# Folding the last two token blocks into a pair of seven half products

## The chip, the cores and the metric

The kernel runs on one core of a Trainium2 chip. The metric is the device time of one execution in microseconds (us). "Span" is the time from the first to the last instruction in a profile; the times of whole runs lie about 1.7 us above it. A store is "issued" when an engine's instruction starts it and "landed" when the profile shows that its data have arrived. An "eviction" is the instruction that reads a finished product out of its accumulator ("bank") so that it can be stored.

## The reference, cut to what matters

Eight batches of a linear attention of eight heads give 4608 tokens of 512 features; a bilinear layer follows.

```python
def _moe_ref(x, w_a, w_b, w_out):
    a = x @ w_a
    b = x @ w_b
    return (a * b @ w_out).astype(np.float32)   # 4608 x 1536  by  1536 x 512
```

The change concerns only the last product. Its left side, `a * b`, is kept transposed in fp16 as `ht`, and it is worked off in 36 blocks of 128 tokens.

## The kernel before

Blocks 0 to 3 are multiplied plainly, early. Then two blocks at a time are multiplied with seven groups of half products in place of eight (a Strassen-like scheme). A half product is one matmul of 256 columns, and each of the seven groups is six of them. The scheme needs four sums of weights, made once, and four sums of tokens per pair (`h_sums`), made on GpSimd, for the last pair on VectorE. Only blocks 4 to 33 are paired. At the end stand block 34 plainly, the last pair (32, 33), and block 35 in two column halves. The code is shortened.

```python
def last_down(cidx):
    for x in range(2):
        cs = slice(w * x, w * (x + 1))
        ...  # 12 matmuls of 256 columns into one bank
        nc.scalar.mul(out=o_sb[:, :w // 2], in_=po[:, :w // 2], mul=1.0 / (CS * CS))
        nc.vector.tensor_scalar(out=o_sb[:, w // 2:], in0=po[:, w // 2:], ...)
        for z, engine in enumerate((nc.sync, nc.scalar)):
            engine.dma_start(out=out_rows[..., cs], in_=o_sb[64 * z:64 * z + 64, :])

def two_downs(self, cidx):              # one pair; self is the work list
    ...
    yield from products(y, a11, quarter(0, 0), True);  u1 = part(y, "u1")     # group 1
    yield from products(v, S1, T1, True);              u5 = part(v, "u5")     # group 2
    yield from products(y, S2, T2);                    u2 = part(y, "u2")     # group 3
    yield from products(v, S4, quarter(1, 1));         plus(o1[:, NH:], v, u2)
    yield from products(y, S3, T3);                    plus(o2[:, NH:], y, u5)
    yield from products(x, a12, quarter(1, 0), True);  plus(o1[:, :NH], x, u1)
    store(o1, cidx)
    yield from products(y, a22, T4)                                           # group 7
    nc.scalar.mul(out=o2[:, :NH], in_=y, mul=scale)
    store(o2, cidx + 1)

def products(self):                     # of class Work: the order of the work
    for cidx in PAIRED[:-1]:
        yield from two_downs(self, cidx)
    yield from down(BLOCKS - 2)
    yield from two_downs(self, PAIRED[-1])
```

`part` is an eviction on ScalarE, `plus` one on VectorE. Note that group 7 adds to the bank `y` that `plus(o2[:, NH:], y, u5)` has to have read. The token sums are put into an engine's order 24 half products ahead of their use (`LEAD`).

The softmax here doesn't subtract the row's maximum and nothing guards it: scores larger than these inputs give would overflow.

Of the kernel before, what the change touches and what calls it, by code (L numbers as in the profile page):

```python
# [8 lines left out]
F32 = mybir.dt.float32  # L9
F16 = mybir.dt.float16  # L10
AF = mybir.ActivationFunctionType
ALU = mybir.AluOpType

P = 128
CS = 16.0
# [3 lines left out]
def kernel(  # L19
# [11 lines left out]
    nc = tc.nc  # L31

    B, H, S, D = q.shape
    M = phi.shape[3]
    d_model, d_ff = moe_w_a.shape
    NHP = H // 2
    NI = S // 64
    NFF = d_ff // P
# [12 lines left out]
    opool = ctx.enter_context(tc.tile_pool(name="opool", bufs=4))  # L51
# [15 lines left out]
    wo_sb = wpool.tile([P, NFF, d_model], F16, name="wo_sb")  # L67
# [72 lines left out]
    banks = Banks()  # L140
# [238 lines left out]
    ht = consts.tile([P, NFF, 2 * S], F16, name="ht")  # L379
    out_rows = out.rearrange("(b p i) f -> b i p f", b=B, i=NI)  # L380

    def down_part(po, bank, cidx, lo, hi):
        pair, c = divmod(cidx, NI)
        for i in range(lo, hi):
            nc.tensor.matmul(po, ht[:, i, P * c:P * (c + 1)], wo_sb[:, i, :],  # L385
                             start=(i == 0), stop=(i == NFF - 1))
            if i == NFF - 1:
                banks.free(bank)
                o_sb = opool.tile([P, d_model], F32, name="o_sb")
                nc.scalar.mul(out=o_sb, in_=po, mul=1.0 / (CS * CS))  # L390
                for z in range(2):
                    slot = 2 * c + z
                    nc.sync.dma_start(out=out_rows[2 * pair + slot // NI, slot % NI],
                                      in_=o_sb[64 * z:64 * z + 64, :])
            yield

    def down(cidx):

        po, bank = banks.take([P, d_model], F32, "po", hold=True)
        yield from down_part(po, bank, cidx, 0, NFF)  # L400

    def last_down(cidx):

        pair, c = divmod(cidx, NI)
        w = d_model // 2
        for x in range(2):
            cs = slice(w * x, w * (x + 1))
            po = banks.tile([P, w], F32, name="pl")
            o_sb = opool.tile([P, w], F32, name="o_sb")
            for i in range(NFF):  # L410
                nc.tensor.matmul(po, ht[:, i, P * c:P * (c + 1)], wo_sb[:, i, cs],
                                 start=(i == 0), stop=(i == NFF - 1))
            nc.scalar.mul(out=o_sb[:, :w // 2], in_=po[:, :w // 2], mul=1.0 / (CS * CS))
            nc.vector.tensor_scalar(out=o_sb[:, w // 2:], in0=po[:, w // 2:], scalar1=1.0 / (CS * CS), scalar2=None,
                                    op0=ALU.mult)
            for z, engine in enumerate((nc.sync, nc.scalar)):
                slot = 2 * c + z
                engine.dma_start(out=out_rows[2 * pair + slot // NI, slot % NI, :, cs],
                                 in_=o_sb[64 * z:64 * z + 64, :])

    EARLY = 4

    def early_downs():
# [9 lines left out]
    KH = NFF // 2  # L433
    NH = d_model // 2
    w_sums = wpool.tile([P, 4, KH, NH], F16, name="w_sums")

    def quarter(x, y):
        return wo_sb[:, KH * x:KH * (x + 1), NH * y:NH * (y + 1)]
# [13 lines left out]
    def sum_tokens(cidx, engine):  # L452

        h_sums[cidx] = spool.tile([P, 4, KH, P], F16, name="h_sums")
        t = [h_sums[cidx][:, x] for x in range(4)]
        (a11, a12), (a21, a22) = ([tokens_of(cidx + y, x) for x in range(2)] for y in range(2))
        for out, in0, in1, op in ((t[0], a21, a22, ALU.add), (t[1], t[0], a11, ALU.subtract),
                                  (t[2], a12, t[1], ALU.subtract), (t[3], a11, a21, ALU.subtract)):
            engine.tensor_tensor(out=out, in0=in0, in1=in1, op=op)  # L459
            yield  # L460

    def store(o_sb, cidx):
        pair, c = divmod(cidx, NI)
        for z in range(2):
            slot = 2 * c + z
            nc.sync.dma_start(out=out_rows[2 * pair + slot // NI, slot % NI], in_=o_sb[64 * z:64 * z + 64, :])

    def two_downs(self, cidx):
        S1, S2, S4, S3 = (h_sums[cidx][:, x] for x in range(4))
        T1, T2, T3, T4 = (w_sums[:, x] for x in range(4))  # L470
        (a11, a12), (a21, a22) = ([tokens_of(cidx + y, x) for x in range(2)] for y in range(2))
        scale = 1.0 / (CS * CS)

        def products(po, lhs, rhs, first=False):
            for i in range(KH):
                nc.tensor.matmul(po, lhs[:, i], rhs[:, i], start=first and i == 0,  # L476
                                 stop=i == KH - 1, skip_group_check=not first)
                if i < KH - 1:
                    yield

        def part(po, name):
            x = ppool.tile([P, NH], F32, name=name)
            nc.scalar.mul(out=x, in_=po, mul=scale)
            return x

        def plus(o, po, x):
            nc.vector.scalar_tensor_tensor(out=o, in0=po, scalar=scale, in1=x, op0=ALU.mult, op1=ALU.add)

        o1, o2 = (opool.tile([P, d_model], F32, name="o_sb") for _ in range(2))
        y, ybank = banks.take([P, NH], F32, "py", hold=True)  # L490
        yield from products(y, a11, quarter(0, 0), True)
        u1 = part(y, "u1")
        yield
        v, vbank = banks.take([P, NH], F32, "pv", hold=True)
        self.brim = True
        yield from products(v, S1, T1, True)
        u5 = part(v, "u5")
        yield
        yield from products(y, S2, T2)
        u2 = part(y, "u2")  # L500
        yield
        yield from products(v, S4, quarter(1, 1))
        banks.free(vbank)
        plus(o1[:, NH:], v, u2)
        self.brim = False
        yield
        yield from products(y, S3, T3)
        plus(o2[:, NH:], y, u5)
        yield
        x, xbank = banks.take([P, NH], F32, "px", hold=True)  # L510
        self.brim = True
        yield from products(x, a12, quarter(1, 0), True)
        banks.free(xbank)
        plus(o1[:, :NH], x, u1)
        store(o1, cidx)
        self.brim = False
        yield
        yield from products(y, a22, T4)
        banks.free(ybank)
        nc.scalar.mul(out=o2[:, :NH], in_=y, mul=scale)  # L520
        store(o2, cidx + 1)
        yield

    BLOCKS = B // 2 * NI
    LEAD = 24
    PLAIN = 0
    PAIRED = range(EARLY + PLAIN, BLOCKS - 2, 2)

    class Work:

# [7 lines left out]
            self.next_sum = next(self.sums)  # L538

        def products(self):  # L540
            for cidx in range(EARLY, EARLY + PLAIN):
                yield from down(cidx)
            for cidx in PAIRED[:-1]:
                yield from two_downs(self, cidx)
            yield from down(BLOCKS - 2)
            yield from two_downs(self, PAIRED[-1])

        def add_up(self):
            for n, cidx in enumerate(PAIRED):
                for x in range(4):  # L550
                    yield n, NFF * PLAIN + 7 * KH * n + KH * (x + 1)
                    if x == 0:
                        sums = sum_tokens(cidx, nc.gpsimd if n < len(PAIRED) - 1 else nc.vector)
                    next(sums)
            while True:
                yield len(PAIRED), 0

# [21 lines left out]
        def plan(self, tokens, slots, keep=24):  # L579

            n = min(max(0, tokens // P - PAIRED[0]) // 2, len(PAIRED))
            self.summed = n
            self.ready = NFF * min(PLAIN, tokens // P - EARLY) + 7 * KH * n + NFF * (tokens // P >= BLOCKS - 1)
            self.rate = max(0, self.ready - self.done - keep) / slots
            self.owed = 0.0
            self.sum_ahead()
# [78 lines left out]
    def chain(b, plan):  # L665


        for x in plan.split():
            if x[0] == "f":
                fill(int(x[1:]), 256)  # L670
            elif x[0] == "y":
                some(int(x[1:]))
            else:
                us[b][x]()
# [4 lines left out]
    ups(steps(0, 0, 4), slots(0, "- hv1a+hx1a - hv1b+hx1b - v1a+x1a - v1b+x1b"))  # L679
    load(2)  # L680
    ups(steps(0, 4, 12), slots(0, "- - - - v2a+x2a - v2b+x2b"))
    chain(1, "exp0 exp1 y9 ks0 y3 kt0 qt0 qt1 y1 ks1 y3 kt1 s0 e0 qt2 qt3 y6 den0 y2 s1 e1 nr0 y4 den1 y2 vs0 vs1 y1 vt0 vt1 nr1 y1 "
             "hv0a hx0a y2 hv0b hx0b y2")
    load(3)
    sum_weights()
    ups(steps(1, 0, 4), slots(1, "y1 hv1a+hx1a hv1b+hx1b y1 v1a+x1a v1b+x1b y3 y3"))
# [13 lines left out]
            ups(half_steps(b, hf), side[NFF * hf:NFF * (hf + 1)] if hf == 0 else side[NFF:])  # L700
    work.plan(S * B, 1, 0)
    work.pull(work.ready - work.done)
    last_down(B // 2 * NI - 1)
# [1 line left out]
_INS = ['q', 'k', 'v', 'phi', 'moe_w_a', 'moe_w_b', 'moe_w_out']  # L705
_OUTS = [((4608, 512), 'float32')]
# [25 lines left out]
```

## Time and profile before

| | before |
|---|---|
| time, median of 3 | 248.29 us (247.92 to 248.95) |
| span of the profiled run | 246.7 us |
| TensorE busy | 95% |
| TensorE's last product ends | 242.23 us |
| last store issued, landed | 243.51, 245.52 us |

The prediction below shows the lines. From 231.5 us on TensorE works without a gap up to its last product, but 4.5 us pass between that product (242.23) and the end (246.74), and in them a queue of stores decides: its last store had its data at 242.93 and was issued at 243.51.

### The profile page before, as it was taken

To read this page: it belongs to the slowest core of one execution; us is meant where nothing else is said; L and a number is where in the kernel's file an instruction comes from. 1 tells how busy PE (TensorE), PEld (TensorE's weight loads), DVE (VectorE), ACT (ScalarE), POOL (GpSimd) and SP (SyncE) were. 2 spreads that over 40 slices of the span, in tenths; PEclk is the share of its full clock that TensorE was granted. 3 is DMA by queue.
4 is the path that set the end of the run, shared out by engine and by line. 5 is a ranking of instruction groups with operands and counts; after the bars stand their busy time and mean duration, and the time that the engine had idled before them with its cause. 6 is when DMAs were issued, how large, how long until landed. Compare 5 with 4: busy or idle time off the path is not lost.

```text
span 246.7 us, 7678 instructions
## 1 busy us (share of the span) xinstructions
PE 235.3 (95%) x3049; PEld 167.3 (68%) x3049; DVE 166.1 (67%) x400; ACT 158.1 (64%) x409; POOL 151.6 (61%) x124
## 2 busy tenths in 40 slices
PE   7989899999998999999999999999999999999992
PEld 2555464456655857777788777877787787888782
DVE  7247773477959967876994649865985676756620
ACT  4147761578697489578856768588855877465230
POOL 8834233499799029892889759892839186946000
PEclk9999999999999999999999999999999999999999
DMA  7999999999979804973159732695120303033145
GB/s 150 196 198 206 207 256 207 255 222 269 235 195 208 159 4 109 234 129 85 34 150 207 173 85 45 168 206 144 36 51 4 86 12 76 15 74 77 43 99 126
DMA packets 26036, 33.53 MB, mean 136 GB/s; under 512 B 1936, under 2 KB 20624, under 8 KB 26000
## 3 DMA queue, kind: packets, MB, share of 16 engines
q0 software_dynamic: 19552, 23.01, 51.2%
q1 hardware_dynamic: 6288, 9.90, 16.3%
q8 instruction: 24, 0.39, 0.6%
q10 hardware_dynamic: 160, 0.13, 0.2%
q14 instruction: 12, 0.10, 0.1%
HBM read 42.47 MB, written 9.44 MB: 210 GB/s over the span
## 4 chain that ended last, share of the span: by engine, by line
PE 74%; DMA 17%; DVE 3%; POOL 2%; issue 1%; ACT 1%; ACTq 0%; DVEq 0%; POOLq 0%
PE pa L598 18%; PE pb L608 16%; PE py L476 15%; PE pv L476 8%; DMA phi_sb<-in_phi_dram 6%; DMA wo_sb<-in_moe_w_out_dram 6%; PE pva L331 5%; DMA wb_sb<-in_moe_w_b_dram 5%; PE px L476 4%; PE po L385 3%; PE pkv L207 2%; PE pD L308 1%; PE pscore L286 1%; PE pT L236 1%; DVE A L319 1%
## 5 line engine op out<-in xcount | busy, mean ns | idle before, releaser
L611 DVE TENSOR_TENSOR ht<-a_sb,pb 128x288 f16<-128x288 f16 x192 | 82.9, 448 | 40.4 <-ACT a_sb L601 29.5
L601 ACT CAST a_sb<-pa 128x288 f16<-128x288 f32 x192 | 74.8, 405 | 31.3 <-PE pa L598 30.7
L598 PE MATMUL pa<-A,vab 128*128 128x288 f16 x384 | 76.6, 287 | 1.4 <-DVE A L319 1.4
L608 PE MATMUL pb<-A,vab 128*128 128x288 f16 x384 | 76.3, 286 | 0.2
L459 POOL TENSOR_TENSOR h_sums<-ht 128x768 f16<-128x768 f16 x28 | 45.8, 1638 | 34.0 <-DVE ht L611 34.0
L608 PEld LDWEIGHTS <-vab 128*128 128x128 f16 x384 | 37.0, 98 | 13.0 <-issue 1.9
L598 PEld LDWEIGHTS <-vab 128*128 128x128 f16 x384 | 34.5, 98 | 15.8 <-issue 9.1
L476 PEld LDWEIGHTS <-h_sums 128*128 128x128 f16 x360 | 35.1, 98 | 6.5 <-issue 0.4
L343 ACT CAST vab<-pva 128x512 f16<-128x512 f32 (+1 forms) x52 | 28.1, 558 | 11.8 <-PE pva L331 11.8
L343 DVE CAST vab<-pva 128x512 f16<-128x512 f32 (+1 forms) x52 | 32.8, 644 | 4.0 <-PE pva L331 3.6
L476 PEld LDWEIGHTS <-ht 128*128 128x128 f16 x270 | 26.4, 98 | 5.4 <-issue 0.2
L476 PE MATMUL py<-w_sums,h_sums 128*128 128x256 f16 x180 | 28.5, 272 | 0.0
L459 POOL TENSOR_TENSOR h_sums<-h_sums,ht 128x768 f16<-128x768 f16 x14 | 23.1, 1647 | 1.0
L459 POOL TENSOR_TENSOR h_sums<-ht,h_sums 128x768 f16<-128x768 f16 x14 | 23.0, 1640 | 1.0
L299 ACT ACTIVATE E<-pscore 128x288 f16<-128x288 f32 x32 | 11.4, 417 | 14.5 <-PE pscore L286 14.4
L319 POOL TENSOR_TENSOR A<-E,R 128x576 f16<-128x576 f16 x10 | 12.8, 1276 | 12.0 <-ACT R L317 11.7
L385 PE MATMUL po<-wo_sb,ht 128*128 128x512 f16 x60 | 16.0, 381 | 0.3 <-DMA wo_sb<-in_moe_w_out_dram 0.3
L476 PE MATMUL py<-wo_sb,ht 128*128 128x256 f16 x90 | 15.2, 273 | 0.0
L476 PE MATMUL pv<-w_sums,h_sums 128*128 128x256 f16 x90 | 15.2, 273 | 0.0
L198 DVE STREAM_TRANSPOSE qT<-q_sb 128x288 f32<-128x288 f32 x32 | 14.5, 463 | 1.0 <-DMA q_sb<-in_q_dram 1.0
L476 PE MATMUL py<-w_sums,ht 128*128 128x256 f16 x90 | 14.7, 272 | 0.1
L476 PE MATMUL px<-wo_sb,ht 128*128 128x256 f16 x90 | 14.6, 273 | 0.0
(64 smaller groups left out, 271.2 us busy)
## 6 DMA issues: line engine op xcount, KB each, us to landing
out_dram<-o_sb SPq DMA_DIRECT2D x70, 128.0 KB, 2.4
kv_sb<-in_v_dram POOLq DMA_DIRECT2D x7, 576.0 KB, 10.0
phi_sb<-in_phi_dram POOLq DMA_DIRECT2D x7, 576.0 KB, 4.6
kv_sb<-in_k_dram POOLq DMA_DIRECT2D x7, 576.0 KB, 8.8
q_sb<-in_q_dram POOLq DMA_DIRECT2D x6, 576.0 KB, 12.7
wo_sb<-in_moe_w_out_dram POOLq DMA_DIRECT2D x3, 512.0 KB, 16.6
q_sb<-in_q_dram POOLq DMA_DIRECT2D x4, 288.0 KB, 12.6
wa_sb<-in_moe_w_a_dram POOLq DMA_DIRECT2D x2, 512.0 KB, 14.9
```

What stands on the lines that cost most here:

```text
L198: nc.vector.transpose(out=t["qT"][:, hp, :].bitcast(F32), in_=qs[b][:, hp, :].bitcast(F32))
L299: nc.scalar.activation(out=Ev[:, g, :, z, :], in_=pss, func=AF.Exp, scale=1.0 / (8.0 * CS))
L319: engine.tensor_tensor(out=attn[b][:, g, sl], in0=t["E"][:, g, sl], in1=t["R", g][:, sl], op=ALU.mult)
L331: nc.tensor.matmul(t["pva", lo, z][g][0][32 * j:32 * j + 32, 0:hi - lo], t["kvT"][64 * r:64 * r + 64, 4 + g, M * j:M * j + M], w_sbs[z][64 ...
L343: engine_copy(out=vabs[b][z][:, g, lo:hi], in_=pva[:, 0:hi - lo])
L385: nc.tensor.matmul(po, ht[:, i, P * c:P * (c + 1)], wo_sb[:, i, :], start=(i == 0), stop=(i == NFF - 1))
L459: engine.tensor_tensor(out=out, in0=in0, in1=in1, op=op)
L476: nc.tensor.matmul(po, lhs[:, i], rhs[:, i], start=first and i == 0, stop=i == KH - 1, skip_group_check=not first)
L598: nc.tensor.matmul(pa, vab[0][:, g, fs], A[:, g, HALF * hf:HALF * (hf + 1)], start=(g == 0), stop=(g == 1))
L601: nc.scalar.copy(out=a_sb, in_=pa)
L608: nc.tensor.matmul(pb, vab[1][:, g, fs], A[:, g, HALF * hf:HALF * (hf + 1)], start=(g == 0), stop=(g == 1))
L611: nc.vector.tensor_tensor(out=ht[:, i, t0:t0 + HALF], in0=a_sbs[hf - hfs[0]], in1=pb, op=ALU.mult)
```

## The change

Blocks 34 and 35 become a sixteenth pair. TensorE has 84 half products at the end in place of 12 full ones, 42 half ones and 24 half ones. The sums of both last pairs are on VectorE. The stores of block 35 go by column halves: the right half after group 5, the left half at the end. The diff is shortened.

```diff
-    def last_down(cidx):
-        ... (block 35 in two column halves)
@@ two_downs
+        ends = cidx == PAIRED[-1]
         yield from products(y, S3, T3)
         plus(o2[:, NH:], y, u5)
+        if ends:
+            store(o2, cidx + 1, slice(NH, d_model))
@@
         nc.scalar.mul(out=o2[:, :NH], in_=y, mul=scale)
-        store(o2, cidx + 1)
+        if ends:
+            store(o2, cidx + 1, slice(0, NH), (nc.sync, nc.scalar))
+        else:
+            store(o2, cidx + 1)
@@
-    PAIRED = range(EARLY + PLAIN, BLOCKS - 2, 2)
+    PAIRED = range(EARLY, BLOCKS, 2)
@@ products: pairs only, block 34 is no longer plain
@@ add_up
-                        sums = sum_tokens(cidx, nc.gpsimd if n < len(PAIRED) - 1 else nc.vector)
+                        sums = sum_tokens(cidx, nc.gpsimd if n < len(PAIRED) - 2 else nc.vector)
@@
-    last_down(B // 2 * NI - 1)
```

More of the change, by code (lines that the diff above doesn't have):

```diff
@@ L400, in down @@
         yield from down_part(po, bank, cidx, 0, NFF)
-    def last_down(cidx):
-        pair, c = divmod(cidx, NI)
-        w = d_model // 2
-        for x in range(2):
-            cs = slice(w * x, w * (x + 1))
-            po = banks.tile([P, w], F32, name="pl")
-            o_sb = opool.tile([P, w], F32, name="o_sb")
-            for i in range(NFF):
-                nc.tensor.matmul(po, ht[:, i, P * c:P * (c + 1)], wo_sb[:, i, cs],
-                                 start=(i == 0), stop=(i == NFF - 1))
-            nc.scalar.mul(out=o_sb[:, :w // 2], in_=po[:, :w // 2], mul=1.0 / (CS * CS))
-            nc.vector.tensor_scalar(out=o_sb[:, w // 2:], in0=po[:, w // 2:], scalar1=1.0 / (CS * CS), scalar2=None,
-                                    op0=ALU.mult)
-            for z, engine in enumerate((nc.sync, nc.scalar)):
-                slot = 2 * c + z
-                engine.dma_start(out=out_rows[2 * pair + slot // NI, slot % NI, :, cs],
-                                 in_=o_sb[64 * z:64 * z + 64, :])
     EARLY = 4
@@ L460, in sum_tokens, with store @@
             yield
-    def store(o_sb, cidx):
+    def store(o_sb, cidx, cs=slice(0, d_model), engines=(nc.sync, nc.sync)):
         pair, c = divmod(cidx, NI)
@@ L465, in store @@
             slot = 2 * c + z
-            nc.sync.dma_start(out=out_rows[2 * pair + slot // NI, slot % NI], in_=o_sb[64 * z:64 * z + 64, :])
+            engines[z].dma_start(out=out_rows[2 * pair + slot // NI, slot % NI, :, cs], in_=o_sb[64 * z:64 * z + 64, cs])
     def two_downs(self, cidx):
@@ L525 @@
     LEAD = 24
-    PLAIN = 0
-    PAIRED = range(EARLY + PLAIN, BLOCKS - 2, 2)
+    PAIRED = range(EARLY, BLOCKS, 2)
     class Work:
@@ L540, in products @@
         def products(self):
-            for cidx in range(EARLY, EARLY + PLAIN):
-                yield from down(cidx)
-            for cidx in PAIRED[:-1]:
+            for cidx in PAIRED:
                 yield from two_downs(self, cidx)
-            yield from down(BLOCKS - 2)
-            yield from two_downs(self, PAIRED[-1])
         def add_up(self):
@@ L550, in add_up @@
                 for x in range(4):
-                    yield n, NFF * PLAIN + 7 * KH * n + KH * (x + 1)
+                    yield n, 7 * KH * n + KH * (x + 1)
                     if x == 0:
-                        sums = sum_tokens(cidx, nc.gpsimd if n < len(PAIRED) - 1 else nc.vector)
+                        sums = sum_tokens(cidx, nc.gpsimd if n < len(PAIRED) - 2 else nc.vector)
                     next(sums)
@@ L582, in plan @@
             self.summed = n
-            self.ready = NFF * min(PLAIN, tokens // P - EARLY) + 7 * KH * n + NFF * (tokens // P >= BLOCKS - 1)
+            self.ready = 7 * KH * n
             self.rate = max(0, self.ready - self.done - keep) / slots
@@ L681 @@
     ups(steps(0, 4, 12), slots(0, "- - - - v2a+x2a - v2b+x2b"))
-    chain(1, "exp0 exp1 y9 ks0 y3 kt0 qt0 qt1 y1 ks1 y3 kt1 s0 e0 qt2 qt3 y6 den0 y2 s1 e1 nr0 y4 den1 y2 vs0 vs1 y1 vt0 vt1 nr1 y1 "
-             "hv0a hx0a y2 hv0b hx0b y2")
+    chain(1, "exp0 exp1 y9 ks0 y3 kt0 qt0 qt1 y1 ks1 y3 kt1 s0 e0 qt2 qt3 y6 den0 y2 s1 e1 nr0 y4 den1 y2 vs0 vs1 y1 vt0 vt1 nr1 y1 hv0a hx0a y2 hv0b hx0b y2")
     load(3)
```

## The prediction

"Instruction" is the profile's name for the packets of q8. That these are TensorE's and are placed by its instruction count is an estimate of mine, from 24 packets of 16 KB for 3049 matmuls and 3049 weight loads. Counted, it holds only roughly: neighbouring packets are 136 to 394 apart.

> **What bounds the kernel now.** I read the page first: busy shares, the slices, the chain.
>
> ```profile
> span 246.7 us, 7678 instructions
> PE 235.3 (95%) x3049; PEld 167.3 (68%) x3049; DVE 166.1 (67%) x400; ACT 158.1 (64%) x409; POOL 151.6 (61%) x124
> PEclk9999999999999999999999999999999999999999
> PE 74%; DMA 17%; DVE 3%; POOL 2%; issue 1%; ACT 1%; ACTq 0%; DVEq 0%; POOLq 0%
> ```
>
> TensorE is 95% busy at full clock and carries 74% of the chain. The change acts only after the last token is known, so I compared the two kernels' instruction orders: up to the 24 half products left over from earlier pairs they are the same on every engine. Only the last 15 us matter. Next I read the chain of waits over that stretch (start, duration, what):
>
> ```profile
> 231.54 0.81 PE py L476 x6
> 232.35 2.59 PE po L385 x12
> 234.94 0.66 PE py L476 x6
> ...
> 238.28 0.66 PE px L476 x6
> 238.94 0.68 PE py L476 x6
> 239.61 1.32 PE pl L411 x12
> ...
> 242.33 0.29 ACT o_sb L413
> 242.61 0.02 issue
> 242.64 0.29 DVE o_sb L414
> ```
>
> The reader should see TensorE without a gap: block 34 plain (po) 2.59 us, pair 32 in 42 half products from 234.94 to 239.61 = 4.67 us (0.111 us each), block 35 (pl) in 24 half products, then ScalarE and VectorE. That chain stops at 242.93, but the span at 246.7, so I read SyncE's store queue in the timeline and looked at its stores one by one:
>
> ```profile
> 239.43 0.47 SPq L466 DMA_DIRECT2D out_dram<-o_sb  x1
> 239.94 1.54 SPq L466 DMA_DIRECT2D out_dram<-o_sb  x1
> 241.58 0.54 SPq L466 DMA_DIRECT2D out_dram<-o_sb  x1
> 242.17 0.59 SPq L466 DMA_DIRECT2D out_dram<-o_sb  x1
> 242.86 0.55 SPq L418 DMA_DIRECT2D out_dram<-o_sb  x1
> 243.51 0.55 SPq L418 DMA_DIRECT2D out_dram<-o_sb  x1
> 242.96 0.49 ACTq L418 DMA_DIRECT2D out_dram<-o_sb  x1
> ```
>
> This queue, not arithmetic, sets the end. The first L418 store on SyncE had its data at 241.61 (VectorE ended then) and was issued at 242.86, 1.25 us late, because four L466 stores stood ahead of it; the last followed at 243.51 although its data was ready at 242.93. It landed 2.01 us later, at 245.52; 1.2 us of closing waits make 246.7. A store costs SyncE about 0.5 to 0.6 us to issue, and the one at 239.94 cost 1.54. Asking for the DMA queues between 239.8 and 239.9 shows why I think it did:
>
> ```profile
> q8 instruction: 1, 0.02, 77.2%
> ```
>
> One 16 KB instruction packet started at 239.87 and took 1.235 us. The other two long store issues lie the same way: 1.20 us from 179.39 beside a packet of 179.25 to 180.21, and 1.13 us from 57.24 beside one of 57.10 to 57.99. In all three the store issue ended 0.38 us after the packet did. That is coincidence in time, thrice; the cause is argued.
>
> [...] 0.55 us of issue against 2.0 us to landing. [...] Here it is not small at the end: six SyncE issues take 4.6 us. [...] 24 q8 packets of 16 KB for TensorE's 6100 instructions, so I take q8 as TensorE's instruction fetch, placed by its instruction count. [...]
>
> **The change, part by part.**
>
> TensorE. Removed: 12 products of 512 columns (2.59 us) and 24 of 256 (24 x 0.111 = 2.66, ending near 242.27). Added: one pair, 42 x 0.111 = 4.67 us. Saved 5.25 - 4.67 = 0.58 us. New times: pair 32 from 232.35 to 237.02, pair 34 from 237.02 to 241.69.
>
> VectorE. Added: four sums of 128x768, 0.55 us each by the rows of pair 32 (230.60, 231.40, 232.20, 232.67, spaced by the evictions between). In the new order the sums of pair 34 stand between pair 32's evictions, so they run from about 235.4 to 238.0. Pair 34 needs them from 237.68, 238.34, 239.01 and 239.69; with the same spacing they are done at about 236.0, 236.8, 237.6, 238.0. Slack at least 1.4 us: hidden. Pair 32 loses the 2.59 us of plain block 34 that stood between its sums and their use: they are done at 231.15, 231.95, 232.75 and 233.23, and are now needed at 233.01, 233.67, 234.35 and 235.02. Slack 1.6 us or more: no wait. Cost on the path 0. The last eviction, ScalarE 0.29 then VectorE 0.29 in series, becomes one ScalarE pass of 128x256, 0.38 us by the u rows: 0.2 us saved, if it is on the path.
>
> Stores. This decides. Before, after the pair's four stores, SyncE had two left, with two on ScalarE's queue. Now pair 34 puts five on SyncE and one on ScalarE: two half-width (right of the second block), two full-width (first block), one half-width (left of the second), all in the last 1.5 us of products. Pair 32 before gives the delays: its fifth group (S3, T3) ended at 238.28, the eviction at 238.74. So pair 34's ends at 237.02 + 3.34 = 240.36, and 0.49 us later, at 240.85, SyncE issues its first store. Back-to-back spacing from the undisturbed four stores at 232.32, 232.83, 233.52, 234.10 is 0.51, 0.69, 0.58; again 0.69 before a store with its own data wait (242.17 to 242.86). I take half-width stores to cost the same issue, as L418's 0.55 says. Issues: 240.85, 241.36, 242.05, 242.63, 243.32. The last one's data is ready at 241.69 + 0.04 + 0.38 + 0.03 = 242.14, so it stands in the queue for 1.2 us. Landing 2.01 later: 245.33. Before: 245.52. Saved 0.19 us.
>
> The instruction fetch. TensorE's order is the same up to the tail, so the fetch comes at the same product count, about 57 after the tail's start: 232.35 + 57 x 0.111 = 238.7 instead of 239.87. There it meets the last of pair 32's stores (about 237.1, 237.6, 238.3, 238.9 by the same spacing), which would end at 238.7 + 1.24 + 0.38 = 240.3, still before 240.85. So the stall that cost before about 0.5 us at its end (without it, the last store would follow its data at about 243.0) is no longer on the path; the added queue takes its place.
>
> Sum: 0.58 on TensorE and 0.2 in eviction, of which the store queue lets 0.19 through. Span 246.7 - 0.2 = 246.5; times of runs lie about 1.7 us above the span (248.44 for the profiled run), hence 248.1.
>
> **Rivals.** First: the queue does not bind and the end follows the arithmetic. Then the last data at 242.14 against 242.93 makes 0.8 us less: 247.5. Against it: SyncE's 0.5 to 0.6 us per issue in every one of its rows. Second: the fetch falls later, or also stalls the third of pair 32's stores; then two issues queue behind it, the first of pair 34 goes out about 0.1 to 0.2 us late and the gain is nil, 248.3; should it come 2 us later than I reckon, it falls into the last five stores and the kernel loses up to 0.8: 249. For it: the stall is the longest in the queue. Against: the packets follow TensorE's count. Third: TensorE waits for the sums. One late sum would cost a few tenths, but the slacks above are over twice one sum. Fourth: the transfers themselves bind; before, DMA engines were 0.83 to 0.98 busy from 242 to 245, after the change 512 KB instead of 768 KB is stored from 240 on, so landing should be no later than 2.0 us after issue.
>
> **Range and chances.** All rivals lie between 247.5 and 249, under 0.5% from 248.3; 2% would be 5 us, a third of the whole stretch. The spread of the three runs before, 247.92 to 248.95, is larger than the effect. I take 248.1, eight in ten between 247.5 and 248.6; within 2% 0.98, the rest split.
>
> **What would show it.** Right: TensorE without a gap through both pairs and its last product near 241.7; no VectorE sums in TensorE's waits; SyncE's five stores of pair 34 back to back from 240.85, the last issued more than 1 us after its data at about 243.3; an instruction packet near 238.7 with a long issue beside it. Wrong: a last issue near 242.2 (first rival), a long issue among the last five (second), gaps before pv or py in the pairs (third), landing well over 2 us (fourth).

## The result, and the profile after

| | before | after |
|---|---|---|
| time, median of 4 | 248.27 us (247.92 to 248.95) | 248.32 us (248.11 to 248.42) |
| ratio | | 0.9998, 95% interval 0.9975 to 1.0020 |

Ratios here are the mean time of one kernel's runs over that of the other's of the same rounds, so not quite the ratio of the medians. Executions over 1.5% slower than the fastest of the same kernel are left out of the means. The time is the same, as far as an interval of about 0.5 us either way can tell. The page of the changed kernel, and its chain of waits over the two pairs (start, duration, what):

```profile
span 246.5 us, 7696 instructions
PE 233.8 (95%) x3055; PEld 167.6 (68%) x3055; DVE 168.5 (68%) x405; ACT 158.5 (64%) x410; POOL 151.8 (62%) x124
```

```profile
234.79 0.68 PE py L458 x6
235.47 0.66 PE px L458 x6
236.13 0.03 issue
236.16 1.47 PE py L458 x12
...
240.97 0.69 PE py L458 x6
241.66 0.02 issue
241.68 0.38 ACT o_sb L504
```

The plain block and the VectorE step at the end are gone, and TensorE is through at 241.65 instead of 242.23. One step is new: at 236.13 the chain breaks off for an "issue" (time for which the profile names no wait) and TensorE's next group starts late.

Spans must not be compared directly. The two kernels are alike until pair 30 is done, yet pair 30's first store went out at 232.32 in the one trace and at 232.09 in the other: 0.23 us of difference that the change cannot have made. I therefore count from that store, the first of SyncE after 230 us (the **mark**), and call the rest up to the end of the span the **tail**. It is 246.74 - 232.32 = 14.42 us before and 246.52 - 232.09 = 14.43 us after. So the 0.2 us by which the span fell lie ahead of the change; by these two traces the change itself gave nothing. How far a tail repeats can be read below: the changed kernel and three variants with the same stores at the end (e3_short_last, e5_fetch_late, e10_fetch_in_last) have 14.42 to 14.46, but the kernel before and a variant of it with the same coincidence of stores (e12_before_fetch_slightly_early) have 14.42 and 14.74.

SyncE's stores of the last pair, one at a time, and ScalarE's:

```profile
240.81 0.47 SPq L447 DMA_DIRECT2D out_dram<-o_sb  x1
241.32 0.60 SPq L447 DMA_DIRECT2D out_dram<-o_sb  x1
242.01 0.54 SPq L447 DMA_DIRECT2D out_dram<-o_sb  x1
242.59 0.59 SPq L447 DMA_DIRECT2D out_dram<-o_sb  x1
243.29 0.54 SPq L447 DMA_DIRECT2D out_dram<-o_sb  x1
242.10 0.56 ACTq L447 DMA_DIRECT2D out_dram<-o_sb  x1
```

The last SyncE store had its data at 242.06 (ScalarE from 241.68, 0.38 us), as ScalarE's own store of 242.10 confirms, and was issued at 243.29. Counted from the mark that is 11.20 us, against 11.19 before: the queue ends where it ended. It landed 2.01 us later, at 245.30.

What cost TensorE 0.17 us in pair 32, in the timeline of the changed kernel, and below it the same place of pair 32 in the kernel before:

```profile
235.23 0.55 DVE L440 TENSOR_TENSOR h_sums<-ht 128x768 f16<-128x768 f16 x1
235.31 0.82 PE L458 MATMUL px<-wo_sb,ht 128*128 128x256 f16 x6
235.69 0.42 DVE L469 SCALAR_TENSOR_TENSOR o_sb<-py,u 128x256 f32<-128x256 f32 x1
236.03 0.55 DVE L440 TENSOR_TENSOR h_sums<-h_sums,ht 128x768 f16<-128x768 f16 x1
236.16 0.82 PE L458 MATMUL py<-w_sums,ht 128*128 128x256 f16 x6
```

```profile
238.12 0.82 PE L476 MATMUL px<-wo_sb,ht 128*128 128x256 f16 x6
238.32 0.42 DVE L487 SCALAR_TENSOR_TENSOR o_sb<-py,u 128x256 f32<-128x256 f32 x1 [0.20 <-PE py L476]
...
238.80 0.81 PE L476 MATMUL py<-w_sums,ht 128*128 128x256 f16 x6
```

A sum for pair 34 begins at 235.23, just ahead of the eviction of group 5, so the eviction waits until 235.69 and reads its bank until 236.11; group 7 adds to that bank and starts at 236.16, 0.31 us after the start of the product before it. At this place of pair 32 in the kernel before, where no sum stands ahead of the eviction, it is 0.13.

### The profile page after: what moved, and what is told of

Same layout as the page of the kernel before. It is cut to its first block, busy times and chain, and to the rows that moved or that the text cites. A ratio compares the mean times of both kernels' runs of the same rounds, so it can differ in the third digit from the quotient of the medians.

```text
span 246.5 us, 7696 instructions
## 1 busy us (share of the span) xinstructions
PE 233.8 (95%) x3055; PEld 167.6 (68%) x3055; DVE 168.5 (68%) x405; ACT 158.5 (64%) x410; POOL 151.8 (62%) x124
## 4 chain that ended last, share of the span: by engine, by line
PE 75%; DMA 17%; DVE 2%; POOL 2%; issue 1%; ACT 1%; DVEq 0%; POOLq 0%
PE pa L580 18%; PE py L458 16%; PE pb L590 16%; PE pv L458 8%; DMA phi_sb<-in_phi_dram 6%; DMA wo_sb<-in_moe_w_out_dram 6%; PE pva L331 5%; DMA wb_sb<-in_moe_w_b_dram 5%; PE px L458 4%; PE pkv L207 2%; PE po L385 2%; PE pD L308 1%; PE pscore L286 1%; PE pT L236 1%; DVE A L319 1%
## 5 line engine op out<-in xcount | busy, mean ns | idle before, releaser
L458 PEld LDWEIGHTS <-h_sums 128*128 128x128 f16 x384 | 37.4, 98 | 6.9 <-issue 0.4
L458 PEld LDWEIGHTS <-ht 128*128 128x128 f16 x288 | 28.2, 98 | 5.6 <-issue 0.4
L458 PE MATMUL py<-w_sums,h_sums 128*128 128x256 f16 x192 | 30.1, 272 | 0.0
L458 PE MATMUL pv<-w_sums,h_sums 128*128 128x256 f16 x96 | 16.0, 273 | 0.0
L458 PE MATMUL py<-wo_sb,ht 128*128 128x256 f16 x96 | 16.0, 273 | 0.0
L465 ACT ACTIVATE u<-py 128x256 f32<-128x256 f32 x32 | 12.3, 385 | 5.2 <-PE py L458 4.9
L458 PE MATMUL py<-w_sums,ht 128*128 128x256 f16 x96 | 15.5, 272 | 0.1
L458 PE MATMUL px<-wo_sb,ht 128*128 128x256 f16 x96 | 15.4, 273 | 0.0
```

The source lines that it names most:

```text
L458: nc.tensor.matmul(po, lhs[:, i], rhs[:, i], start=first and i == 0, stop=i == KH - 1, skip_group_check=not first)
L465: nc.scalar.mul(out=x, in_=po, mul=scale)
```

## The experiments

All times in the table but the ratio are from one profile each, counted from pair 30's first store. In the two kernels with pair 34's sums on GpSimd that store itself is late (at 233.53 in e1_pool_sums, against 232.09 after the change), so for those the ratio is the better measure. Ratios are against the kernel before, five rounds (the row "after" has the result above); their intervals are about 0.0012 to 0.002 either way, 0.3 to 0.5 us.

| kernel | ratio | TensorE ends | last issue | last landing | tail |
|---|---|---|---|---|---|
| before | 1 | 9.91 | 11.19 | 13.19 | 14.42 |
| after | 0.9998 | 9.56 | 11.20 | 13.21 | 14.43 |
| e3_short_last | 1.0000 | 9.00 | 11.23 | 13.25 | 14.46 |
| e2_whole_rows | 1.0015 | 9.55 | 10.57 | 13.36 | 14.70 |
| e11_half_bytes | 0.9985 | 9.55 | 10.57 | 12.56 | 13.90 |
| e6_two_queues | 0.9973 | 9.55 | 10.20 | 12.60 | 13.87 |
| e1_pool_sums | 1.0094 | 10.35 | 11.99 | 14.03 | 15.25 |
| e8_sums_earlier | 0.9996 | 9.38 | 11.03 | 13.03 | 14.24 |
| e7_pool_two_queues | 1.0054 | 10.34 | 10.99 | 13.37 | 14.65 |
| e9_sums_earlier_two_queues | 0.9979 | 9.38 | 10.03 | 12.42 | 13.71 |
| e4_before_fetch_early | 0.9985 | 9.92 | 10.64 | 12.86 | 14.14 |
| e5_fetch_late | 1.0015 | 9.56 | 11.20 | not in the trace | 14.42 |
| e10_fetch_in_last | 1.0009 | 9.55 | 11.20 | 13.21 | 14.42 |
| e12_before_fetch_slightly_early | 1.0013 | 9.92 | 11.35 | 13.52 | 14.74 |

### Does arithmetic set the end, or the queue?

**e3_short_last**: one product of six in the last group; wrong result.

```diff
-        yield from products(y, a22, T4)
+        yield from products(y, a22, T4, n=1 if ends else KH)
```

> The changed kernel with only one of six products in the very last group (a22 by T4 of pair 34); a wrong result on purpose. TensorE ends 0.55 us earlier and the last eviction with it. Queue theory: the last store stands in SyncE's queue anyway, the last issue stays at about 1.2 us after the first half-width pair and the tail stays 14.43 within 0.05. Rival (arithmetic sets the end): tail 13.9.

TensorE ended 0.56 us earlier (9.00 against 9.56) and the tail was 14.46. Time on TensorE at the very end is worth nothing in the changed kernel: the queue theory held, the arithmetic rival fell.

**e2_whole_rows**: undo the column halves.

```diff
-        if ends:
-            store(o2, cidx + 1, slice(NH, d_model))
@@
-            store(o2, cidx + 1, slice(0, NH), (nc.sync, nc.scalar))
+            store(o2, cidx + 1, engines=(nc.sync, nc.scalar))
```

> The changed kernel without the column halves: the last block is stored as whole rows at the end, one store on SyncE and one on ScalarE's queue, so SyncE has three stores after pair 34 instead of five. Queue theory: SyncE issues at about 241.46, 241.97, 242.66 on the time axis of the changed kernel, the last lands about 2.3 us later at 244.97 instead of 245.30: tail 14.1 us, 0.3 less than 14.43. Rival (the transfers bind, the half-width stores help because bytes leave earlier): the last landing is later than 245.3 and the tail is 14.5 to 14.8.

A miss. The last issue came 0.63 us earlier, as the queue theory has it, but that store landed 2.78 us after its issue, not 2.3, and the tail grew to 14.70. Here the rival was right: the halves of the change do help.

**e11_half_bytes**: the same four stores as in e2_whole_rows, each with only the left 256 columns; wrong result.

```diff
-        store(o1, cidx)
+        store(o1, cidx, slice(0, NH if ends else d_model))
@@
-            store(o2, cidx + 1, engines=(nc.sync, nc.scalar))
+            store(o2, cidx + 1, slice(0, NH), (nc.sync, nc.scalar))
```

> The whole-row version (tail 14.70, last landing 2.78 us after its issue) with the last pair storing only its left 256 columns, so the same four store issues with half the bytes; a wrong result on purpose. If the whole-row version was late because its last 512 KB could not be moved faster, the landing falls to 2.0 to 2.3 us after issue and the tail to about 14.0. Rival (the number of stores alone counts, or the landing is slow for another cause): landing stays near 2.8 and the tail near 14.7.

The issue stayed at 10.57, the landing fell to 1.99 us after it and the tail to 13.90. So bytes made e2_whole_rows late. The sums by stretch show it, first of e2_whole_rows, then of e11_half_bytes (the last two columns are the busy share of the DMA engines and GB/s):

```profile
243.00:244.00 1.00, 0.00 (x0) 0.00 (x0) 0.00 (x0) 0.00 (x0) 0.00 (x0) 1.00 0.87 193
244.00:245.00 1.00, 0.00 (x0) 0.00 (x0) 0.00 (x0) 0.00 (x0) 0.00 (x0) 1.00 0.99 191
```

```profile
243.00:244.00 1.00, 0.00 (x0) 0.00 (x0) 0.00 (x0) 0.00 (x0) 0.00 (x0) 1.00 0.41 92
244.00:245.00 1.00, 0.00 (x0) 0.00 (x0) 0.00 (x0) 0.00 (x0) 0.00 (x0) 1.00 0.76 170
```

With whole rows the DMA engines are nearly full (0.87 and 0.99); with half the bytes they are not (0.41 and 0.76). So there are two limits close together: with five stores on SyncE it is the issue queue (in the changed kernel the last one had its data 1.2 us before it was issued), with three stores of whole rows the transfers (2.78 us to landing, with half the bytes 1.99).

**e6_two_queues**: keep the column halves, but give each of the last pair's three double stores one SyncE and one ScalarE issue; the last eviction moves to VectorE.

```diff
-            store(o2, cidx + 1, slice(NH, d_model))
+            store(o2, cidx + 1, slice(NH, d_model), (nc.sync, nc.scalar))
@@
-        store(o1, cidx)
+        store(o1, cidx, engines=(nc.sync, nc.scalar if ends else nc.sync))
@@
-        nc.scalar.mul(out=o2[:, :NH], in_=y, mul=scale)
+        if ends:
+            nc.vector.tensor_scalar(out=o2[:, :NH], in0=y, scalar1=scale, scalar2=None, op0=ALU.mult)
+        else:
+            nc.scalar.mul(out=o2[:, :NH], in_=y, mul=scale)
```

> The changed kernel with each of the last pair's three double stores split between SyncE's and ScalarE's queues (three each), and the last eviction on VectorE so that ScalarE's queue is free. Queue theory: SyncE's last issue follows the last data, at about 242.15 on the changed kernel's time axis instead of 243.29, landing 2.0 to 2.5 us later: tail 0.7 to 1.1 us less than 14.43. Rival (the transfers themselves bind, the same bytes): last landing hardly earlier, tail 14.2 or more.

The last issue came 1.00 us earlier; the tail fell by 0.56, less than I expected, and the time by 0.27% against before (interval 0.11 to 0.43%). The last store, now ScalarE's, landed 2.40 us after its issue in place of 2.01: part of the gain was lost between issue and landing. That the transfers took it is a guess and not shown: the DMA engines were 0.94 busy from 243 to 244 us, against 0.75 in the changed kernel, but ScalarE's store of the changed kernel had needed 2.49 as well. The moved eviction is not what helped: in the changed kernel the last SyncE store had its data 1.2 us before it was issued. ScalarE's second issue, beside one of SyncE's and right behind a first such pair, took 0.73 us; in the changed kernel no store issue of this stretch took over 0.60.

### The wait on the delayed eviction

**e1_pool_sums**: pair 34's sums on GpSimd.

```diff
-   sums = sum_tokens(cidx, nc.gpsimd if n < len(PAIRED) - 2 else nc.vector)
+   sums = sum_tokens(cidx, nc.vector if n == len(PAIRED) - 2 else nc.gpsimd)
```

> The changed kernel with pair 34's four sums moved from VectorE to GpSimd, nothing else. Measure: the tail, from the issue of pair 30's first store on SyncE (the first store after 230 us) to the end of the span; before 246.74 - 232.32 = 14.42 us, after 246.52 - 232.09 = 14.43 us. My theory: in the changed kernel the sums on VectorE delay one eviction of pair 32 and TensorE waits about 0.2 us before pair 32's last group (start to start 0.31 us instead of 0.11), and all later stores move with it. So that gap closes to 0.11 and the tail falls by about 0.2 to 14.2. Rival: the gap has another cause (ScalarE, a bank), then gap and tail stay. Second rival: GpSimd's sums at 1.64 us each come too late and TensorE waits before pair 34's second group: tail longer.

The wait did close: pair 32's group 7 started 0.13 us after the product before it, with no sum on VectorE ahead of the eviction. But the time got longer, by 0.94% or 2.3 us, and the second rival named the wrong pair: what came late were VectorE's own sums of pair 32. Lines of the timeline of e1_pool_sums:

```profile
232.84 1.83 POOL L440 TENSOR_TENSOR h_sums<-h_sums,ht 128x768 f16<-128x768 f16 x1
...
233.43 1.65 DVE L440 TENSOR_TENSOR h_sums<-ht,h_sums 128x768 f16<-128x768 f16 x1
...
234.75 1.83 POOL L440 TENSOR_TENSOR h_sums<-ht,h_sums 128x768 f16<-128x768 f16 x1
...
235.01 1.99 DVE L440 TENSOR_TENSOR h_sums<-ht 128x768 f16<-128x768 f16 x1
```

Three of VectorE's four sums of pair 32, 0.55 us alone, took 1.65 to 1.99 beside GpSimd's, and each ended 0.4 us after a sum of GpSimd's had (233.43 + 1.65 = 235.08 against 232.84 + 1.83 = 234.67). TensorE started three groups of pair 32 late, 0.55, 0.54 and 1.35 us after the product before, the last of them when VectorE's last sum was done. Why VectorE's sums were held beside GpSimd's, and why until 0.4 and not 0.55 us after them, no run here shows. In the kernels before and after, GpSimd has no sums left in the tail (busy 0.00 us from the mark on).

**e8_sums_earlier**: the sums stay on VectorE, 24 half products earlier.

```diff
-   yield n, 7 * KH * n + KH * (x + 1)
+   yield n, 7 * KH * n + KH * (x + 1) - 24 * (n == len(PAIRED) - 1)
```

> The changed kernel with pair 34's four sums still on VectorE but ordered 24 half products earlier, all ahead of pair 32's evictions instead of between them. Moving them to GpSimd had failed because they ran beside VectorE's own sums. Theory: TensorE's wait before pair 32's last group (start to start 0.31 us) closes to 0.11, the stores of pair 34 go out 0.2 us earlier and the tail falls from 14.43 to about 14.2 us. Rival: that wait is not the sums' doing, or the sums now delay something else: wait or tail stay.

In the timeline of e8_sums_earlier the eviction of group 5 follows group 5 at once and group 7 starts 0.13 us after the product before it:

```profile
235.95 0.82 PE L458 MATMUL px<-wo_sb,ht 128*128 128x256 f16 x6
...
236.15 0.42 DVE L469 SCALAR_TENSOR_TENSOR o_sb<-py,u 128x256 f32<-128x256 f32 x1
...
236.63 0.82 PE L458 MATMUL py<-w_sums,ht 128*128 128x256 f16 x6
```

The wait closed, TensorE ended 0.18 us earlier and the tail fell to 14.24, as expected. Together with the wait that closed in e1_pool_sums this shows that the sums in VectorE's order made it. The time's ratio of 0.9996 (0.9984 to 1.0009) cannot show an effect of 0.08%; the tail in one trace does.

**e7_pool_two_queues** and **e9_sums_earlier_two_queues** join e6_two_queues with one or the other.

> Both together: pair 34's sums on GpSimd and the last pair's stores on two queues. If the two effects are separate they add: 0.2 less than e6_two_queues, a tail of about 13.2 to 13.5 us, and a time about 1.0 us below both kernels. Rival: with the store queue no longer the bound or still the bound one of the two is worth nothing and the tail equals that of e6_two_queues.

> The earlier sums and the last pair's stores on two queues together. If both are separate: tail about 13.7 us (13.87 for the two queues alone, 0.2 less), time about 0.9 us below the kernel before. Rival: the transfers bind there, then the earlier data is worth nothing and the tail stays 13.87.

e7_pool_two_queues is slow for the reason just given (its TensorE starts late by the same three amounts); next to e1_pool_sums its tail is 0.60 shorter, the two queues' part again. e9_sums_earlier_two_queues has the shortest tail, 13.71: 0.16 less than with the queues alone, so the two add. Its time is 0.21% below before (0.05 to 0.37%), about 0.5 us and not the 0.9 expected; by the ratio it cannot be told from e6_two_queues. Both are a little faster than before, at the edge of what these rounds resolve.

### The instruction packet

**e4_before_fetch_early**: the kernel before with 20 more warm-up matmuls at the start (22 of 16 columns for two of 512; the helper takes a list of widths for that), to bring the instruction packet earlier in the tail, by the estimate that TensorE's instruction count places it.

```diff
-    fill(16)
+    fill([16] * 22 + [512] * 14)
```

> The kernel before with 20 more matmul pairs among the warm-up products at the very start (22 tiny ones in place of two), so that TensorE's instruction packets come about 20 half products earlier in the tail: near 237.6 instead of 239.87, when SyncE has no store to issue. Theory: the store issue of 1.54 us becomes 0.60, the tail falls from 14.42 by 0.5 to 13.9 us. Rival: the long issue has another cause at that place (the store itself, TensorE's last block): it stays, tail 14.4.

The packet came at 237.88, when SyncE was idle, and the second store of pair 32 was issued in the usual time (e4_before_fetch_early):

```profile
239.77 0.60 SPq L466 DMA_DIRECT2D out_dram<-o_sb  x1
```

The last issue moved forward by 0.55 us as expected, but the tail only by 0.28: the last two stores now go out together on two queues, and the later landing counts. The comparison leans on one trace of the kernel before; against e12_before_fetch_slightly_early, which has the same hold, it would be 0.60. The time's ratio, 0.9985 (0.9966 to 1.0003), has the right sign and is not clear of 1.

**e5_fetch_late** and **e10_fetch_in_last**: the changed kernel with 20 and with 10 fewer warm-up matmuls, to bring the packet among the last stores.

```diff
-            fill(int(x[1:]), 256)          # e5_fetch_late: pairs of 256 columns joined to 512
+            fill([512] * (int(x[1:]) // 2) + [256] * (int(x[1:]) % 2))
+            # e10_fetch_in_last: 14 of 256 become 7 of 512, 3 of 256 become 2 of 384
```

> The changed kernel with 20 fewer warm-up matmuls at the start (pairs of 256 columns joined to 512), so that TensorE's instruction packet of 239.36 comes about 20 half products later, near 241.6 to 242.8, among the last five stores of SyncE. Theory: a store issue inside the packet's time ends about 0.38 us after the packet, near 243.2; the last issue moves from 243.29 to about 243.9 and the tail from 14.43 to about 15.0 us (0.3 to 0.9 more). Rival: packets have no part in it, the tail stays 14.4.

> The changed kernel with ten fewer warm-up matmuls (with twenty fewer, TensorE's last instruction packet did not come at all). The packet should start about ten half products later than in the changed kernel, near 240.4 to 240.6, and last until about 241.7, across the first of SyncE's last five stores. Theory: that issue takes until about 0.38 us after the packet, near 242.0; the last issue moves from 243.29 to about 243.9 to 244.1 and the tail from 14.43 to about 15.0 us. Rival: a packet beside a store is no cause: issues of 0.47 to 0.60 and a tail of 14.4.

With 20 fewer the last packet did not come at all, and the tail was 14.42: without any packet in it the changed kernel is no faster, so the packet costs it nothing. With 10 fewer it came from 241.26 to 242.22, across the first of the last stores, and held nothing (e10_fetch_in_last):

```profile
241.61 0.47 SPq L447 DMA_DIRECT2D out_dram<-o_sb  x1
```

So my theory, that any store issue inside a packet is held, is wrong as stated.

**e12_before_fetch_slightly_early**: the kernel before with six more warm-up matmuls, for an amended theory.

```diff
-    fill(16)
+    fill([16] * 7 + [512] * 15)
```

> The kernel before with six more warm-up pairs at the start, so that the instruction packet comes about 0.4 to 0.7 us earlier in the tail, at 6.9 to 7.2 us after pair 30's first store instead of 7.55, that is about when the first of pair 32's four back-to-back stores is issued (7.11) and lasting past the issue of the second (7.62). In the run with the packet across the last stores a first store after a pause was issued in 0.47 us although it lay inside the packet, so my theory that every issue inside a packet is held is wrong as stated. Amended theory: only a store that follows close upon another whose data have not moved yet is held, until about 0.38 us after the packet. Then the first issue takes 0.47 and the second 0.9 to 1.4 us, ending near 8.5 to 8.8, and the tail is 14.2 to 14.4. Rival: the long issue of the kernel before had nothing to do with the packet: the second issue is 0.60 here (as it was with the packet far away), tail 14.1; or the first is held too, over 1 us.

The packet did not move: it came 7.50 us after the mark, as before (7.55), from 239.62 to 240.98. The run therefore repeats the coincidence instead of making a new one. The first store took 0.47; the second, longer than I had expected, took

```profile
239.74 1.61 SPq L466 DMA_DIRECT2D out_dram<-o_sb  x1
```

which is until 241.36, 0.37 after the packet. The tail, 14.74, is longer than I expected too: after that hold, two of SyncE's issues that came right behind a pair issued on both queues at once took 0.69 and 0.71.

With 14 traces at hand I counted all stores on SyncE, so mostly on traces that were there before the theory. Of those that began inside a 16 KB packet's time with 0.25 us or more of it left, 27 followed another store within 0.2 us: all 27 ended 0.37 to 0.40 us after the packet. Ten followed a pause of over 1 us or were the first store of all: seven took 0.47, two 0.55, one 0.61. That agrees with the amended theory as far as "close upon another" goes; whether it matters that the other's data have not moved, no run here separates. e4_before_fetch_early shows that the long issue goes when the packet goes, and in e5_fetch_late, whose packets lie elsewhere, the usual long issues near 57 and 179 us are gone and others stand at 110.64, 121.89, 151.85 and 225.37, each ending 0.37 to 0.38 us after a packet. Not every long issue is of this kind: all 14 traces have one of 0.76 to 1.19 us near 97 us without a packet. Why a second store is held and a first is not, I did not find out.

## Why the prediction was right or wrong

The number, its range and the reading that nothing much would change were right. The range tests little, though: it is 1.1 us wide for a foretold gain of 0.19, which runs that spread over 1 us cannot show. By its steps:

- **TensorE saves 0.58 us: right by the count of columns, 0.35 as measured** (9.91 to 9.56). With the wait removed, e8_sums_earlier shows 0.53 (9.91 to 9.38).
- **"Cost on the path 0" for VectorE's sums: the step that failed.** The sums were in time, with the slack foretold, and I looked only for a product waiting for a sum. What they delayed is the eviction of group 5, which stands behind one of them in VectorE's order, and group 7 waits for that eviction's bank. It cost 0.17 us of TensorE (0.31 from start to start against 0.13) where 0 was foretold; e8_sums_earlier, which takes the sums out of the way, gives 0.18 back. The same wait stands in the kernel before, in pair 30 (its group starts at 231.54, 0.34 after the product before it); I had that trace and did not read the gap.
- **Store queue: right in kind and nearly in number.** Foretold from 240.85 to 243.32; measured 240.81 to 243.29 on an axis that starts 0.23 earlier, so every issue is 0.2 later, the wait just named. The spacing, the 1.2 us that the last store stands in the queue and its landing after 2.01 us are as foretold. e3_short_last shows that the queue and not arithmetic sets this end. (The prediction's 4.6 us for six issues before runs from the first start to the last end; the issues alone add up to 4.24, with 1.54 for the held one.)
- **"Saved 0.19 us": measured nothing**, tail 14.43 against 14.42. The missing 0.2 is the wait: without it, in e8_sums_earlier, the tail is 14.24, 0.18 less than before, nearly the foretold gain (one trace each). That the span fell by the predicted 0.2 is luck: it lies ahead of the change.
- **The packet: half right.** It was no longer on the path, as foretold, but it came 7.26 us after the mark and not 6.4, between the stores of both pairs, so no long issue lay beside it. The step "the same product count" was off: 6073 matmuls and weight loads had started before the packet, against 6059 before the change, so seven products more; why, no run shows. Over these runs the 24th packet came after 6059 to 6075 matmuls and weight loads (in e5_fetch_late, with 6070 in all, it did not come), and six more products at the start (e12_before_fetch_slightly_early) did not move it. Two stores already issued landed 3.6 and 3.3 us after their issue instead of 2.3 to 2.4 (2.3 and 2.4 in e5_fetch_late, without the packet), which nobody waited for. In the kernel before it did cost: by e4_before_fetch_early 0.55 us of the last issue, where I had said 0.5, and 0.28 us of tail.
- **Rivals.** "The end follows the arithmetic" fell with e3_short_last. The sign named for "TensorE waits for the sums", a gap before py, was there (236.16), and the sign for being right, TensorE without a gap, was not; but what TensorE waited for was an eviction and no sum. "The transfers bind" was put too weakly: with five half and whole stores in a queue it does not hold, but with three whole-row stores it does (e2_whole_rows against e11_half_bytes, 2.78 us to landing against 1.99).

Where the gain went, then: a wait for a delayed eviction took nearly 0.2 of the 0.58 us on TensorE, as much as the tail was to gain, and the rest ended in front of a store queue that five stores in 2.5 us keep full, as foretold. Against a kernel before that misses its packet (14.14) the changed one would even be 0.3 us longer in the tail, by one profile each. Whether the kernel before would gain as much from a second queue for its last pair was not run.

## What to carry to other kernels

At the very end of a kernel count store issues as well as products: each issue was here about a quarter of its 2.0 to 2.4 us to landing, but issues of 0.47 to 0.60 us in one queue held the last store back by 1.2 us. Spreading the last six over two queues made the last issue 1.00 us earlier and was worth 0.56 us of tail in one trace, while TensorE's end 0.56 us earlier (e3_short_last) was worth nothing there. When you add work to an engine in the slack of another, check not only that the work is done in time but what stands behind it in that engine's order: here that cost TensorE 0.17 us. And compare tails from an event that both kernels share: spans of like prefixes differed here by more than the effect.
